# Attention scores and softmax weights turned by VectorE's 32x32 block transposes instead of TensorE's

## The chip, the core and the metric

The kernel runs on one core of one Trainium2 chip. The metric is the device time of one execution in microseconds (us), as the median of several runs. Abbreviations are those of the profile: PE is TensorE (PEld its weight loads), DVE is VectorE, ACT is ScalarE, POOL is GpSimd, SP is SyncE, which issues the DMAs. L12 is line 12 of the kernel.

## The reference

A packed attention is followed by two feed-forward layers. With 8 batches, 8 heads, 576 tokens, 64 features a head and 32 packed queries:

```
sm_attn(qq, kk, vv): s = scale * qq @ kk^T;  s -= max(s);  a = exp(s);  a /= sum(a) + 1e-9;  return a @ vv
p_packed = sm_attn(p, k, v)                      # 32 rows a head
out      = sm_attn(q, p_packed, p_packed)        # 576 rows a head, 32 columns of scores
x = out as (4608 tokens, 512)
x = x / rms(x) * rms_g;  x = (silu(x @ w_gate) * (x @ w_val)) @ w_out     # 512 -> 1536 -> 512
h = x @ w_in;  result = (h * cos(h)) @ w_out2                             # 512 -> 2048 -> 512
```

The second attention has 32 scores for each head and token, and its softmax runs over those 32. The change is about that softmax.

## The kernel before

**Stages.** First come 16 packing units (two a batch, four heads each), which compute `p_packed` from k, v and p, and load and narrow the weights beside it (the L143 to L153 operations on tiles `wy` and `ny`). From its fifth unit on, this stage also carries the second attention of batch 0. Then the first feed-forward layer runs batch by batch, 24 half-blocks a batch: `gv` is gate and value of 128 features for 288 tokens (12 matmuls, three for each product, since each operand is split into a high and a low part), `acc` adds the product with `w_out` (6 matmuls, three half-blocks later). Between the half-blocks of batch b lies the second attention of batch b+1. The last batch has no attention beside it. Then comes the second feed-forward layer (`hp`, `ops`).

**The attention** of a batch is a generator, `attend`, that yields between small steps. For each group g of four heads it turns q on TensorE (`qtp`), multiplies by the packed rows (`sp`, 128 rows of head and packed query x 288 tokens, one tile for even and one for odd tokens), and copies the two tiles out (`sT`, one by ScalarE, one by VectorE). It turns them on TensorE (`stp`, blocks of 96 tokens x 128), takes maxima over 32 scores (`amx`) and subtracts. After both groups `s` holds 96 partitions x 1536; two exponentials, then two rounds of sum, reciprocal and scaling (`sm`) work on halves of 768 columns. Then the weights are turned back by TensorE, four blocks of three transposes (`atp`), each copied by ScalarE into `at`. The steps x (products `xp` and squares for the norm), r, b and p follow.

**What sets the order.** The program is written out by hand in these two stages. In the packing stage each unit takes up to three steps of `attend(0)`, `ATT_U` in all. In the feed-forward layer `att_step` takes steps in proportion: `N_ATT` steps over the 48 half-steps of a batch. After the softmax the order of steps is a string, `ATT_ORD` (`ATT_ORD0` for batch 0), in which `t` turns weights, `x`, `r`, `b`, `p` are as above and `-` is an empty step:

```
ATT_ORD = "t00 t10 - x00 t01 t11 - x10 - - r00 - - b00 b10 p00 p10"
ATT_ORD0 = "t00 t10 x00 x01 t01 t11 x10 x11 - r00 - b00 b10 p00 p10"
```

The matmul outputs of attention, of `gv` and of `unit` (tile `mps`, which makes the folded weights `wmhl` of a batch) share one PSUM pool: `psb[0]`, two buffers in the packing stage and four in the feed-forward layer. ScalarE holds one table of functions at a time: silu and exp need a table load (ACT_TABLE_LOAD) between them.

Of the kernel before, what the change touches and what calls it, by code (L numbers as in the profile page):

```python
# [9 lines left out]
F32 = mybir.dt.float32  # L10
F32R = mybir.dt.float32r
I32 = mybir.dt.int32  # L12
AF = mybir.ActivationFunctionType
# [7 lines left out]
def kernel(  # L21
# [14 lines left out]
    nc = tc.nc  # L36
# [28 lines left out]
    W_FROM, W_TO = 1, 16  # L65
    W_ORD = (0, 1, 2, 3, 16, 4, 5, 6, 17, 7, 8, 18, 9, 10, 11, 19, 12, 13, 14)
    W_KV = 16
    ATT_U, U_ATT = 31, 5
    S_PAD = 11
    U_S = {6: 0, 10: 1, 14: 2}  # L70
    U_AT = {3: (0, 3), 8: (0, 4), 14: (0, 5), 16: (1, 0), 18: (1, 1), 20: (1, 2), 22: (1, 3), 26: (1, 4), 30: (1, 5)}
# [6 lines left out]
    T_END, F3_B, OWN = 2, 3, 16  # L78
    LAG, LAG_B = 3, 4

    ATT_ORD = "t00 t10 - x00 t01 t11 - x10 - - r00 - - b00 b10 p00 p10"
    ATT_ORD0 = "t00 t10 x00 x01 t01 t11 x10 x11 - r00 - b00 b10 p00 p10"
    AL_AT, CL_AT = 16, 21
    ATT_FROM, ATT_TO, ATT_FROM0, ATT_TO0, N_ATT = 0, 48, 10, 45, 37
    BX, BS, BW = 10, 13, 12

    wide = w_gate.dtype != F32
# [128 lines left out]
        nc.sync.dma_start(out=cl, in_=c_dram[b])  # L216

    def attend(b):
        s = a1.tile([CP, NC_, H, NP], F32, tag="s", name="s")
        for g in range(2):  # L220
            qTs = []
            for j in (2 * g, 2 * g + 1):
                qv = qn.pop(4 * b + j)
                qT = a2.tile([128, 2, HALF], F32, tag="qT", name="qT")
                for i in range(2):
                    tp = psb[0].tile([128, HALF], F32, tag="mm", name="qtp")
                    for c in range(CH):
                        nc.tensor.transpose(  # L228
                            tp[:, c * CP:(c + 1) * CP], qv[:, i, 2 * c:2 * c + 2, :].rearrange("p c d -> p (c d)"),
                            ident[:CP, :CP],  # L230
                        )
                    nc.scalar.activation(out=qT[:, i], in_=tp, func=AF.Copy)
                    qTs.append(qT[:, i])
                    if i == 0:
                        yield
                load_q()
                yield
            sp = [psb[0].tile([128, HALF], F32, tag="mm", name="sp") for _ in range(2)]
            for h in range(4):
                for r, rows in enumerate((top, bot)):  # L240
                    nc.tensor.matmul(
                        sp[r][h * NP:(h + 1) * NP], bq[rows, 4 * g + h], qTs[h][rows], start=True, stop=True
                    )
            sT = a1.tile([128, 2, HALF], F32, tag="sT", name="sT")
            nc.scalar.activation(out=sT[:, 0], in_=sp[0], func=AF.Copy)
            nc.vector.tensor_copy(sT[:, 1], sp[1])
            yield
            for r in range(2):
                st_p = psb[0].tile([CP, CH, 4, NP], F32, tag="mm", name="stp")
                for c in range(CH):  # L250
                    nc.tensor.transpose(
                        st_p[:, c].rearrange("p h n -> p (h n)"), sT[:, r, c * CP:(c + 1) * CP], ident
                    )
                mx = a2.tile([CP, CH, 4], F32, tag="amx", name="amx")
                nc.vector.tensor_reduce(out=mx, in_=st_p, op=ALU.max, axis=AX.X)
                nc.vector.tensor_tensor(
                    out=s.rearrange("p (c t) h n -> p c t h n", t=2)[:, :, r, 4 * g:4 * g + 4, :], in0=st_p,
                    in1=mx.unsqueeze(3).to_broadcast([CP, CH, 4, NP]), op=ALU.subtract,
                )
            yield  # L260
        n_s = 8 * CH
        hv = [s[:, hf * CH:(hf + 1) * CH].rearrange("p c h n -> p (c h) n") for hf in range(2)]
        for sf in hv:
            nc.scalar.activation(out=sf, in_=sf, func=AF.Exp, scale=scale)
            yield "e"
        for sf in hv:
            sm = a2.tile([CP, 2, n_s], F32, tag="sm", name="sm")
            nc.vector.tensor_reduce(out=sm[:, 0], in_=sf, op=ALU.add, axis=AX.X)
            nc.vector.tensor_scalar(out=sm[:, 0], in0=sm[:, 0], scalar1=1e-9, scalar2=None, op0=ALU.add)
            nc.vector.reciprocal(out=sm[:, 1], in_=sm[:, 0])  # L270
            yield
            if b:
                yield
            nc.vector.tensor_tensor(
                out=sf, in0=sf, in1=sm[:, 1].unsqueeze(2).to_broadcast([CP, n_s, NP]), op=ALU.mult
            )
            yield

        def transposed(hf, kt):
            tp = psb[0].tile([128, HALF], F32, tag="mm", name="atp")  # L280
            for c in range(CH):
                nc.tensor.transpose(
                    tp[:, c * CP:(c + 1) * CP],
                    s[:, hf * CH + c, 4 * kt:4 * kt + 4, :].rearrange("p h n -> p (h n)"), ident[:CP, :CP],
                )
            return tp

        z = {}

        def a_t(hf, kt):  # L290
            if (hf, kt) == (0, 0):
                z["at"] = a1.tile([128, 2, 2, HALF], F32, tag="at", name="at")
            nc.scalar.activation(out=z["at"][:, kt, hf], in_=transposed(hf, kt), func=AF.Copy)

        def a_x(kt, part):
            at = z["at"]
# [708 lines left out]
    def o_out(n, t):  # L1005
# [8 lines left out]
        while off < 128:  # L1014
            if n < B:
                b, u = n, t * 128 + off
            else:
                b, u = divmod(t * 128 + off, REST)
                u += TOK
            c, pp = divmod(u, CP)  # L1020
            m = min(128 - off, CP - pp)
            dst = out[b * S:(b + 1) * S].rearrange("(p c) d -> c p d", c=NC_)[c, pp:pp + m, :]
            nc.sync.dma_start(out=dst, in_=ob[off:off + m])
# [57 lines left out]
```

## Time and profile before

| | |
|---|---|
| median of 3 runs | 1689.0 us (1687.13 to 1690.26) |
| span of the profiled execution, first to last instruction | 1681.2 us |
| TensorE busy | 1628.8 us, 97% of the span |
| VectorE busy | 1008.5 us, 60% |
| ScalarE busy | 845.2 us, 50% |
| GpSimd busy | 73.9 us, 4% |

The profiled execution has a time of its own only as its span; the runs' times take in what lies around the span. Busy time of matmuls is modelled from starts, as they are pipelined: where the distance between two starts matters, the timeline shows it. A shape such as 96x384 is partitions x elements. "Idle before" is the time the engine stood still just ahead of the instructions of a group, and the arrow names what ended it. The granted clock is TensorE's, as a share of full speed.

### The profile page before, as it was taken

The page shows a single profiled execution, that of the slowest core. Times are in us where ns is not written, and L with a number is a line of the kernel's source. Part 1 is how long each engine was busy: PE and PEld are TensorE (multiplying, and loading weights), DVE is VectorE, ACT ScalarE, POOL GpSimd, SP SyncE. Part 2 cuts the span into 40 slices and gives each one's busy share as a digit, 9 for nine tenths or more (in the row PEclk, how much of TensorE's full clock was granted, in tenths as well). Part 3 has the DMA queues.
Part 4 walks back from the last instruction along what each step waited for, and adds up shares of the span by engine and source line. Part 5 has one row for each costly group of instructions (what it writes and reads, how often), then busy time and mean ns, then how long its engine had stood idle before and what let it go on. Part 6 is the DMA issues. An engine that isn't in the chain of part 4 may idle for free.

```text
span 1681.2 us, 26128 instructions
## 1 busy us (share of the span) xinstructions
PE 1628.8 (97%) x10112; PEld 1325.8 (79%) x10112; DVE 1008.5 (60%) x1890; ACT 845.2 (50%) x1587; POOL 73.9 (4%) x74
## 2 busy tenths in 40 slices
PE   7877999999999999999999999999999999999998
PEld 5545868788888788888888888888888888888887
DVE  3577985566565666665435665656565656565554
ACT  4455555455454545454434554545454545454443
POOL 1001430000000000000110000000000000000000
PEclk9887999999999999999999999999999999999999
DMA  9996744454535454544363020101010101000001
GB/s 253 285 247 173 226 158 153 145 183 139 195 120 179 143 176 144 170 127 131 104 239 106 25 63 1 51 1 51 0 50 1 50 1 41 11 0 26 1 26 25
DMA packets 103580, 177.35 MB, mean 105 GB/s; under 512 B 39456, under 2 KB 55840, under 8 KB 103456
## 3 DMA queue, kind: packets, MB, share of 16 engines
q1 hardware_dynamic: 103456, 175.68, 34.4%
q8 instruction: 80, 1.31, 0.3%
q14 instruction: 44, 0.36, 0.1%
HBM read 134.22 MB, written 41.42 MB: 104 GB/s over the span
## 4 chain that ended last, share of the span: by engine, by line
PE 89%; DMA 5%; DVE 3%; ACT 1%; issue 1%; SPq 1%; POOL 0%; DVEq 0%; POOLq 0%; ACTq 0%
PE hp L160 8%; PE hp L159 8%; PE hp L158 8%; PE ops L160 8%; PE ops L159 8%; PE ops L158 8%; PE gv L158 6%; PE acc L158 6%; PE gv L159 6%; PE gv L160 6%; PE acc L160 6%; PE acc L159 6%; PE mps L580 3%; DMA kn<-in_k_dram 2%; PE qtp L228 1%
## 5 line engine op out<-in xcount | busy, mean ns | idle before, releaser
L158 PE MATMUL gv<-apt,wmhl 128*128 128x288 f32 x768 | 237.8, 310 | 3.0 <-DVE silu L766 2.0
L159 PE MATMUL gv<-apt,wmhl 128*128 128x288 f32 x768 | 228.6, 298 | 0.2 <-DVE apt L107 0.2
L160 PE MATMUL gv<-apt,wmhl 128*128 128x288 f32 x768 | 228.0, 297 | 0.0
L159 PE MATMUL hp<-xhl,wmhl 128*128 128x512 f32 x576 | 224.1, 389 | 0.0
L160 PE MATMUL hp<-xhl,wmhl 128*128 128x512 f32 x576 | 224.1, 389 | 0.0
L158 PE MATMUL ops<-w2hl,ghl 128*128 128x512 f32 x576 | 224.1, 389 | 0.0
L159 PE MATMUL ops<-w2hl,ghl 128*128 128x512 f32 x576 | 224.1, 389 | 0.0
L158 PE MATMUL hp<-xhl,wmhl 128*128 128x512 f32 x576 | 223.9, 389 | 0.0
L160 PE MATMUL ops<-w2hl,ghl 128*128 128x512 f32 x576 | 222.3, 389 | 0.0
L981 ACT ACTIVATE r<-r 128x512 f32<-128x512 f32 x144 | 91.1, 633 | 250.0 <-DVE r L980 250.0
L989 DVE TENSOR_TENSOR r<-r,hp 128x512 f32<-128x512 f32 x144 | 98.9, 687 | 164.8 <-ACT r L982 164.8
L158 PEld LDWEIGHTS gv<-apt,wmhl 128*128 128x128 f32 x768 | 146.0, 190 | 44.3 <-issue 17.6
L158 PE MATMUL acc<-shl,wohl 128*128 128x512 f32 x432 | 176.6, 409 | 0.2 <-DMA shl<-s 0.2
L160 PE MATMUL acc<-shl,wohl 128*128 128x512 f32 x432 | 170.7, 395 | 2.4 <-POOL wohl L546 2.4
L159 PE MATMUL acc<-shl,wohl 128*128 128x512 f32 x432 | 169.6, 393 | 0.0
L773 ACT ACTIVATE shl<-silu 128x288 fp32r<-128x288 f32 x192 | 85.4, 445 | 159.6 <-DVE silu L766 158.4
L766 DVE TENSOR_TENSOR silu<-silu,gv 128x288 f32<-128x288 f32 x192 | 86.5, 451 | 125.5 <-PE gv L160 106.2
L976 ACT ACTIVATE kk<-hp,magic 128x512 f32<-128x512 f32 x144 | 99.1, 688 | 117.3 <-PE hp L160 117.1
L159 PEld LDWEIGHTS gv<-apt,wmhl 128*128 128x128 f32 x768 | 146.2, 190 | 4.4 <-DVE apt L107 0.5
L160 PEld LDWEIGHTS gv<-apt,wmhl 128*128 128x128 f32 x768 | 145.8, 190 | 0.0
L977 DVE TENSOR_SCALAR kk<-kk 128x512 f32<-128x512 f32 x144 | 61.4, 426 | 116.1 <-ACT kk L976 116.0
L158 PEld LDWEIGHTS ops<-w2hl,ghl 128*128 128x128 f32 x576 | 108.2, 188 | 22.6
(127 smaller groups left out, 2708.4 us busy)
## 6 DMA issues: line engine op xcount, KB each, us to landing
wy<-wy SPq DMA_DIRECT2D x96, 512.0 KB, 4.5
kn<-in_k_dram SPq DMA_DIRECT2D x16, 576.0 KB, 7.4
vn<-in_v_dram SPq DMA_DIRECT2D x48, 192.0 KB, 6.5
qnat<-in_q_dram SPq DMA_DIRECT2D x32, 288.0 KB, 4.1
x_dram<-x SPq DMA_DIRECT2D x18, 512.0 KB, 3.0
x1raw<-x_dram SPq DMA_DIRECT2D x18, 512.0 KB, 4.0
raw<-in_moe_w_in_dram SPq DMA_DIRECT2D x16, 512.0 KB, 4.2
raw<-in_moe_w_out_dram SPq DMA_DIRECT2D x16, 512.0 KB, 4.2
```

The source lines that it names most:

```text
L158: nc.tensor.matmul(ps, lhi, rhi, start=first, stop=False)
L159: nc.tensor.matmul(ps, lhi, rlo, start=False, stop=False)
L160: nc.tensor.matmul(ps, llo, rhi, start=False, stop=last)
L228: nc.tensor.transpose(tp[:, c * CP:(c + 1) * CP], qv[:, i, 2 * c:2 * c + 2, :].rearrange("p c d -> p (c d)"), ident[:CP, :CP],)
L580: nc.tensor.matmul(ps[kt][h * NP:(h + 1) * NP], ppT[b // 4][rows, 4 * kt + h, n:n + NP], w_y[2 * u + kt][rows, j], start=True, stop=True,)
L766: nc.vector.tensor_tensor(out=t, in0=t, in1=pss[1], op=ALU.mult)
L773: nc.scalar.activation(out=sh[:, 0, cols], in_=t, func=AF.Copy)
L976: nc.scalar.activation(out=kk, in_=hp, func=AF.Identity, scale=1.0 / TWO_PI, bias=magic[:, 0:1])
L977: nc.vector.tensor_scalar(out=kk, in0=kk, scalar1=-MAGIC, scalar2=None, op0=ALU.add)
L981: nc.scalar.activation(out=r, in_=r, func=AF.Abs)
L989: nc.vector.tensor_tensor(out=r, in0=r, in1=hp, op=ALU.mult)
```

## The change

The score tiles stay with 128 rows. VectorE's transpose works inside blocks of 32 x 32: a tile of 128 rows (4 heads x 32 packed queries) x 288 tokens becomes one whose partition is head and token-within-block and whose columns are block and packed query. So the 32 scores of a head and token stand side by side on one partition, and the softmax runs on 128 partitions x 576 for each group. One exponential covers both groups (128 x 1152). The same transpose turns the weights back into `at`, whose columns then hold the even tokens and then the odd ones; the output's row mapping follows (line with `CH` in `o_out`). TensorE's `stp` and `atp` and the copies `sT` and `at` are gone. The steps of the generator become 28 (batch 0, before its last two) and 32.

```diff
-    ATT_U, U_ATT = 31, 5
+    ATT_U, U_ATT = 28, 5
-    ATT_ORD = "t00 t10 - x00 t01 t11 - x10 - - r00 - - b00 b10 p00 p10"
-    ATT_ORD0 = "t00 t10 x00 x01 t01 t11 x10 x11 - r00 - b00 b10 p00 p10"
+    ATT_ORD = "t00 - x00 t10 - x10 - - r00 - - b00 b10 p00 p10"
+    ATT_ORD0 = "t00 x00 x01 t10 x10 x11 - r00 - b00 b10 p00 p10"
-    ATT_FROM, ATT_TO, ATT_FROM0, ATT_TO0, N_ATT = 0, 48, 10, 45, 37
+    ATT_FROM, ATT_TO, ATT_FROM0, ATT_TO0, N_ATT = 0, 48, 10, 45, 32
...
-        s = a1.tile([CP, NC_, H, NP], F32, tag="s", name="s")
+        NB = HALF // NP
+        s = a1.tile([128, 2, 2, NB, NP], F32, tag="s", name="s")
...
-            sT = a1.tile([128, 2, HALF], F32, tag="sT", name="sT")
-            nc.scalar.activation(out=sT[:, 0], in_=sp[0], func=AF.Copy)
-            nc.vector.tensor_copy(sT[:, 1], sp[1])
+            st = a2.tile([128, 2, NB, NP], F32, tag="st", name="st", bufs=1)
+            for r in range(2):
+                nc.vector.transpose(st[:, r].rearrange("p c n -> p (c n)"), sp[r])
             yield
-            for r in range(2):
-                st_p = psb[0].tile([CP, CH, 4, NP], F32, tag="mm", name="stp")
-                for c in range(CH):
-                    nc.tensor.transpose(
-                        st_p[:, c].rearrange("p h n -> p (h n)"), sT[:, r, c * CP:(c + 1) * CP], ident
-                    )
-                mx = a2.tile([CP, CH, 4], F32, tag="amx", name="amx")
-                nc.vector.tensor_reduce(out=mx, in_=st_p, op=ALU.max, axis=AX.X)
...
+            mx = a2.tile([128, 2 * NB], F32, tag="amx", name="amx")
+            nc.vector.tensor_reduce(out=mx, in_=sv, op=ALU.max, axis=AX.X)
+            nc.vector.tensor_tensor(
+                out=s[:, g].rearrange("p r c n -> p (r c) n"), in0=sv,
+                in1=mx.unsqueeze(2).to_broadcast([128, 2 * NB, NP]), op=ALU.subtract,
+            )
             yield
-        for sf in hv:
-            nc.scalar.activation(out=sf, in_=sf, func=AF.Exp, scale=scale)
-            yield "e"
-        for sf in hv:
-            sm = a2.tile([CP, 2, n_s], F32, tag="sm", name="sm")
+        nc.scalar.activation(out=s, in_=s, func=AF.Exp, scale=scale)
+        yield "e"
+        for g in range(2):
+            sf = s[:, g].rearrange("p r c n -> p (r c) n")
+            sm = a2.tile([128, 2, 2 * NB], F32, tag="sm", name="sm")
...
-            if b:
-                yield
...
-        def a_t(hf, kt):
-            if (hf, kt) == (0, 0):
+        def a_t(kt, _):
+            if kt == 0:
                 z["at"] = a1.tile([128, 2, 2, HALF], F32, tag="at", name="at")
-            nc.scalar.activation(out=z["at"][:, kt, hf], in_=transposed(hf, kt), func=AF.Copy)
+            nc.vector.transpose(
+                z["at"][:, kt].rearrange("p r x -> p (r x)"), s[:, kt].rearrange("p r c n -> p (r c n)")
+            )
...
+            c = 2 * (c % CH) + c // CH
```

How instructions move is shown at three places; a row is one instruction or a run of equal ones, with output, inputs and output shape. First TensorE in the feed-forward layer of batch 1, at the score product of batch 2's first group. Before:

```order
L241 MATMUL sp<-qT,bq 32x288 x8
L158 MATMUL acc<-shl,wohl 128x512
L159 MATMUL acc<-shl,wohl 128x512
L160 MATMUL acc<-shl,wohl 128x512
L158 MATMUL acc<-shl,wohl 128x512
L159 MATMUL acc<-shl,wohl 128x512
L160 MATMUL acc<-shl,wohl 128x512
L251 MATMUL stp<-ident,sT 96x128 x6
L158 MATMUL gv_3366<-apt,wmhl 128x288
```

After:

```order
L158 MATMUL acc<-shl,wohl 128x512
L159 MATMUL acc<-shl,wohl 128x512
L160 MATMUL acc<-shl,wohl 128x512
L158 MATMUL acc<-shl,wohl 128x512
L159 MATMUL acc<-shl,wohl 128x512
L160 MATMUL acc<-shl,wohl 128x512
L242 MATMUL sp<-qT,bq 32x288 x8
L158 MATMUL gv_3270<-apt,wmhl 128x288
```

`stp` is gone, and `sp` has moved from ahead of the `acc` block to behind one. Second ScalarE in the same loop, at the exponential of batch 2. Before, from the first exponential's table load:

```order
L264 ACT_TABLE_LOAD
L264 ACTIVATE s<-s 96x768
L773 ACTIVATE shl<-silu 128x288
L765 ACT_TABLE_LOAD
L765 ACTIVATE silu<-gv_3611 128x288
```

After:

```order
L750 ACTIVATE silu<-gv_3477 128x288
L758 ACTIVATE shl<-silu 128x288
L257 ACT_TABLE_LOAD
L257 ACTIVATE s<-s 128x1152
L750 ACT_TABLE_LOAD
L750 ACTIVATE silu<-gv_3503 128x288
```

Before, such a sequence stands twice in a batch, once for each half; after, it stands once, and the copy `shl` has moved ahead of it. Third the packing stage, TensorE at the last units that carry batch 0's attention (`pp` ends a unit's packing product, `et` and `s` open the next one's). Before:

```order
L282 MATMUL atp<-ident,s 128x96 x3
L460 MATMUL pp<-vn,eT 32x64 x24
L302 MATMUL xp<-at,cl 64x288 x8
L446 MATMUL et<-ident,e 128x128 x6
L423 MATMUL s_1641<-kT,pT 32x288 x8
```

After:

```order
L445 MATMUL pp<-vn,eT 32x64 x24
L287 MATMUL xp<-at,cl 64x288 x4
L431 MATMUL et<-ident,e 128x128 x6
L408 MATMUL s_1503<-kT,pT 32x288 x8
```

and VectorE beside it, after (`cd` reads `pp`, `at` is read by `xp`):

```order
L266 TENSOR_TENSOR s<-s,sm 128x576
L449 TENSOR_SCALAR cd<-pp,mx 128x128
L276 STREAM_TRANSPOSE at<-s 128x576
L297 TENSOR_TENSOR ssq<-ssq,sq 128x288
L143 TENSOR_SCALAR ny<-ny 128x512
```

The turn of the weights has moved from TensorE, a unit step ahead of `xp`, to VectorE, behind `cd` and directly ahead of `xp`.

## Rows read from the trace of the kernel before

**Rows 1.** Busy time by stretch: start:end, length, engines, granted clock, DMA share, GB/s.
```profile
100.00:165.00 65.00, 44.86 (x568) 31.20 (x569) 46.26 (x108) 34.05 (x81) 2.88 (x4) 0.76 0.72 202
165.00:265.00 100.00, 93.65 (x683) 72.85 (x681) 82.21 (x146) 55.12 (x120) 39.22 (x25) 0.98 0.57 178
265.00:805.00 540.00, 540.00 (x3996) 441.59 (x3988) 328.87 (x690) 279.12 (x591) 9.51 (x6) 1.00 0.48 155
```
**Rows 2.** TensorE's groups, 265 to 805 us: busy us, mean ns, idle before.
```profile
L158 PE MATMUL gv<-apt,wmhl 128*128 128x288 f32 x592 | 182.4, 308 | 0.0
...
L282 PE MATMUL atp<-ident,s 96*128 96x96 f32 x72 | 9.9, 245 | 0.0
L251 PE MATMUL stp<-ident,sT 128*96 128x128 f32 x72 | 9.8, 272 | 0.0
```
**Rows 3.** TensorE's timeline from 724 us: start, duration, instruction (L159, L160 left out).
```profile
724.77 0.82 PE L251 MATMUL stp<-ident,sT 128*96 128x128 f32 x6
725.34 0.38 PE L158 MATMUL gv<-apt,wmhl 128*128 128x288 f32 x1
...
727.01 0.39 PE L158 MATMUL acc<-shl,wohl 128*128 128x512 f32 x1
...
728.40 0.29 PE L158 MATMUL gv<-apt,wmhl 128*128 128x288 f32 x1
...
729.99 0.40 PE L158 MATMUL acc<-shl,wohl 128*128 128x512 f32 x1
...
744.45 0.41 PE L282 MATMUL atp<-ident,s 96*128 96x96 f32 x3
744.64 0.38 PE L158 MATMUL gv<-apt,wmhl 128*128 128x288 f32 x1
...
746.32 0.41 PE L282 MATMUL atp<-ident,s 96*128 96x96 f32 x3
```
**Rows 4.** VectorE's groups by shape, whole span.
```profile
L255 DVE TENSOR_REDUCE amx<-stp 96x12 f32<-96x384 f32 x32 | 17.6, 548 | 12.7 <-PE stp L251 12.7
...
L274 DVE TENSOR_TENSOR s<-s,sm 96x768 f32<-96x768 f32 x16 | 15.2, 948 | 0.0
...
L268 DVE TENSOR_REDUCE sm<-s 96x24 f32<-96x768 f32 x16 | 15.1, 941 | 0.0
...
L334 DVE TENSOR_TENSOR at<-at,rb 128x576 f32<-128x576 f32 x16 | 11.7, 749 | 0.0
...
L246 DVE COPY sT<-sp 128x288 f32<-128x288 f32 x16 | 7.2, 451 | 1.0 <-PE sp L241 1.0
...
L270 DVE RECIPROCAL sm<-sm 96x24 f32<-96x24 f32 x16 | 4.8, 299 | 0.6
...
L269 DVE TENSOR_SCALAR sm<-sm 96x24 f32<-96x24 f32 x16 | 3.1, 193 | 0.5
```
**Rows 5.** ScalarE's groups by shape, 265 to 805 us.
```profile
L264 ACT ACT_TABLE_LOAD x12 | 15.4, 1283 | 0.2
...
L264 ACT ACTIVATE s<-s 96x768 f32<-96x768 f32 x12 | 10.2, 848 | 0.1
L293 ACT ACTIVATE at<-atp 128x288 f32<-128x288 f32 x24 | 9.8, 410 | 5.2 <-PE atp L282 5.1
```
**Rows 6.** Timeline from 197 us, ScalarE's silu and TensorE's waits (in brackets).
```profile
197.01 0.41 ACT L765 ACTIVATE silu<-gv 128x288 f32<-128x288 f32 x1 [1.32 <-PE gv L160]
...
203.14 0.41 ACT L765 ACTIVATE silu<-gv 128x288 f32<-128x288 f32 x1
...
209.31 0.44 PE L282 MATMUL atp<-ident,s 96*128 96x96 f32 x3 [1.32 <-ACT silu L765]
...
212.80 0.61 PE L158 MATMUL gv<-apt,wmhl 128*128 128x288 f32 x1 [2.03 <-DVE silu L766]
```
**Rows 7.** Waits, 100 to 168 us: who for whom, us in total, times, longest.
```profile
PE xp L302 <- ACT at L293: 3.5, 2, 2.0
PE mps L580 <- ACT sq L311: 3.5, 1, 3.5
```

More of the change, by code (lines that the diff above doesn't have):

```diff
@@ L243, in attend @@
                     )
-            sT = a1.tile([128, 2, HALF], F32, tag="sT", name="sT")
-            nc.scalar.activation(out=sT[:, 0], in_=sp[0], func=AF.Copy)
-            nc.vector.tensor_copy(sT[:, 1], sp[1])
+            st = a2.tile([128, 2, NB, NP], F32, tag="st", name="st", bufs=1)
+            for r in range(2):
+                nc.vector.transpose(st[:, r].rearrange("p c n -> p (c n)"), sp[r])
             yield
-            for r in range(2):
-                st_p = psb[0].tile([CP, CH, 4, NP], F32, tag="mm", name="stp")
-                for c in range(CH):
-                    nc.tensor.transpose(
-                        st_p[:, c].rearrange("p h n -> p (h n)"), sT[:, r, c * CP:(c + 1) * CP], ident
-                    )
-                mx = a2.tile([CP, CH, 4], F32, tag="amx", name="amx")
-                nc.vector.tensor_reduce(out=mx, in_=st_p, op=ALU.max, axis=AX.X)
[L256 to L259, printed above, removed]
-            yield
-        n_s = 8 * CH
-        hv = [s[:, hf * CH:(hf + 1) * CH].rearrange("p c h n -> p (c h) n") for hf in range(2)]
-        for sf in hv:
-            nc.scalar.activation(out=sf, in_=sf, func=AF.Exp, scale=scale)
-            yield "e"
-        for sf in hv:
-            sm = a2.tile([CP, 2, n_s], F32, tag="sm", name="sm")
+            sv = st.rearrange("p r c n -> p (r c) n")
+            mx = a2.tile([128, 2 * NB], F32, tag="amx", name="amx")
[4 more added lines that the diff above has]
+            )
+            yield
+        nc.scalar.activation(out=s, in_=s, func=AF.Exp, scale=scale)
[3 more added lines that the diff above has]
+            sm = a2.tile([128, 2, 2 * NB], F32, tag="sm", name="sm")
             nc.vector.tensor_reduce(out=sm[:, 0], in_=sf, op=ALU.add, axis=AX.X)
@@ L271, in attend @@
             yield
-            if b:
-                yield
             nc.vector.tensor_tensor(
-                out=sf, in0=sf, in1=sm[:, 1].unsqueeze(2).to_broadcast([CP, n_s, NP]), op=ALU.mult
+                out=sf, in0=sf, in1=sm[:, 1].unsqueeze(2).to_broadcast([128, 2 * NB, NP]), op=ALU.mult
             )
             yield
[L279 to L286, printed above, removed]
         z = {}
-        def a_t(hf, kt):
-            if (hf, kt) == (0, 0):
+        def a_t(kt, _):
+            if kt == 0:
                 z["at"] = a1.tile([128, 2, 2, HALF], F32, tag="at", name="at")
-            nc.scalar.activation(out=z["at"][:, kt, hf], in_=transposed(hf, kt), func=AF.Copy)
+            nc.vector.transpose(
+                z["at"][:, kt].rearrange("p r x -> p (r x)"), s[:, kt].rearrange("p r c n -> p (r c n)")
+            )
         def a_x(kt, part):
```

## The prediction

> **What bounds the kernel now.** I read the table of stretches first, since a share over the whole span mixes stages [rows 1]. It shows three regimes ahead of the second feed-forward layer. From 100 to 165 us (end of the packing units, in which batch 0's attention runs) no engine is full: TensorE 44.9 of 65 us, VectorE 46.3, granted clock 0.76. From 165 to 265 us (feed-forward layer of batch 0, with batch 1's attention in between) VectorE is busy 82.2 of 100 us and TensorE 93.7. From 265 to 805 us (batches 2 to 7's attention) TensorE is busy 540.0 of 540 us at a granted clock of 1.00, VectorE 328.9 and ScalarE 279.1.
>
> A busy TensorE is modelled, so the second view is the groups of that stretch with their idle time: the feed-forward matmuls and both transposes that go waited 0.0 us [rows 2]. The third is the timeline, which gives starts. A block of 12 gv matmuls straight after acc takes 728.40 to 729.99, 1.59 us, or 0.13 us each; the starts follow at one distance, without a gap [rows 3].
>
> The Trainium skill (Perfetto Trace Analysis, section Identifying the Most-Contended Engine) speaks against reading this as a bound: busy time of matmuls is no good measure of headroom, because they are pipelined. That rule is weighed by the starts in rows 3, which show back-to-back work; if it nevertheless meant slack here, the sum below would be zero, which is the second rival.
>
> **TensorE's part, step by step.** Two groups go: in each batch 12 score transposes (stp, two blocks of 6) and 12 weight transposes (atp, four blocks of 3); the counts of 72 over six batches in [rows 2] agree. Their durations, 272 and 245 ns, are latencies; what they hold of a full engine is the distance of starts [rows 3]:
> - stp: 724.77 to 725.34 is 0.57 us for six. The gv block behind it takes 725.34 to 727.01, 1.67 us against 1.59: coming back to the feed-forward matmuls costs 0.08 us more. Together 0.65 us.
> - atp: 744.45 to 744.64 is 0.19 us for three, and the gv block behind takes 744.64 to 746.32, 1.68 us: 0.09 more. Together 0.28 us.
>
> A batch thus gives back 2 x 0.65 + 4 x 0.28 = 2.42 us. Six batches lie where TensorE is the bound: 6 x 2.42 = 14.5 us. The q transposes, score products, xp and rb stay in number; in the order some move to the other side of an acc block, which I cost at nothing: as many returns to the feed-forward matmuls remain.
>
> By the Trainium skill (TensorE: Matmul & The Clock Gate, Part 4: PE-mode transpose) a transpose costs about 275 ns in a kernel's context, most of it memory latency. The latency agrees with the 272 ns of rows 2, but charged per instruction it would make 24 x 0.275 = 6.6 us a batch, an estimate from that page; the starts in rows 3 decide for 2.42.
>
> **VectorE's part.** From [rows 4], per batch: out go two score copies (2 x 0.45), four maxima (4 x 0.55), four subtractions (about as long, 4 x 0.55), two sums (2 x 0.94), two scalings (2 x 0.95), together 9.1 us. In come operations on 128 partitions x 576 instead of 96 x 768 or 96 x 384: two maxima, subtractions, sums and scalings, eight at the 0.75 us of the 128x576 row, 6.0 us. Unknown are the transposes: four of 128x288 from PSUM and two of 128x576. No row has one. Low end: what an operation on 24 elements takes, 0.19 us each, 1.2 us in all. High end: the slowest rate per element in the trace, RECIPROCAL against TENSOR_SCALAR on the same 24 elements, (299 - 193)/24 = 4.4 ns above a base of 0.19, giving 0.19 + 288 x 0.0044 = 1.5 us and 2.7 us, so 4 x 1.5 + 2 x 2.7 = 11.4 us. I take the copy of the same shape from PSUM, 0.45, and the 128x576 row, 0.75: 3.3 us, since a transpose without arithmetic streams its columns as a copy does. VectorE ends at 9.3 us a batch, 0.2 more than now; at the high end 8.3 more. In 265 to 805 us that is 6 x 8.3 = 50 us on top of 329 of 540: still not the bound, so there the cover is VectorE's free 39%.
>
> **ScalarE's part.** It loses two score copies and four weight copies (0.41 each, [rows 5]), and two exponentials of 0.85 become one of 128x1152, about 0.85 x 1152/768 = 1.27 us. An exponential between silu's forces two table loads of 1.28 us [rows 5]; in batches 2 to 7 the two exponentials stand on either side of a silu, so four loads become two. All this is hidden now (TensorE waits for nothing in that stretch), so I cost it at nothing there. Against it: the loads and the exponential stand in one piece, 1.28 + 1.27 + 1.28 = 3.8 us against 3.4, and silu behind them frees the PSUM buffers of gv. Counted from the end of a gv block: silu, VectorE's product and the copy take about 0.41 + 0.45 + 0.41 = 1.3 us, the piece lasts until 5.1, the next silu and product until 6.0. That next gv block ended at 1.39 + 1.59 = 2.98, and its buffers are wanted two blocks on, at 2 x 2.98 + 1.39 = 7.35 us. That leaves 1.3 us; today's shorter piece causes no wait.
>
> **Batch 1 (165 to 265 us).** TensorE gives back the same 2.42 us. Here VectorE binds for a while: TensorE waits 1.32 us at 209.31 and 2.03 us at 212.80, the second for VectorE's silu product; on ScalarE no silu ran from 197.4 to 203.1, while both exponentials and their table loads did [rows 6]. In the new order one exponential follows a silu directly and the copy and reload come behind it: between two silu's 1.28 + 1.27 + 0.41 + 1.28 = 4.2 us, against those 5.7. I take 1.4 us of the difference off the 3.35 us wait. The softmax pieces on VectorE are also 0.2 us shorter each, while the two at transposes come later, where it has room; I count neither. Together 3.8 us. At the high end of the transposes four slow ones fall into the full stretch, 4 x 1.05 = 4.2 us later.
>
> **Stage to 165 us (batch 0).** No engine is full behind 100 us, so chains decide [rows 1]. New: the at transposes stand on VectorE behind cd, which needs pp of the same unit, and TensorE's xp stands right behind pp; it waits for cd and the transpose, at least 0.75 us, in two units. Queued behind xp are the et transposes and the packing scores; their maximum comes on VectorE only after four or more narrowing operations on 128x512, each longer than the 0.45 us of a 128x288 copy, so over 1.8 us, which cover the wait. Without that cover it costs 1.5 us, and 3 with as much again for cd and what queues ahead. Gone: xp's waits for the ScalarE copies, 3.5 us, and mps's wait behind the squares, 3.5 us [rows 7], as mps no longer stands right behind four xp. If a good half of these 7 was on the chain, 4 us go. I take the middle, about 0, between -4 and +3; at the high end of the transposes 2 x 1.95 = 3.9 more.
>
> **The sum.** -14.5 - 3.8 + 0 = -18.3 us. The profiled execution spans 1681.2 us, so 1662.9; the median of the runs is 1689.0, 7.8 above that span, for what lies around it and for differences between executions; I carry that over: 1670.7 us.
>
> **Rivals.**
> 1. The transposes are slow. For: no row shows one. Against: VectorE has room from 265 us on. Time at the high end: -18.3 + 4.2 + 3.9 = -10.2, 1678.8 us; with stage one at its own worst 1682.
> 2. TensorE is not what holds the end: other waits fill the freed time and it goes the same, 1689 us. For: the 3.35 us wait of batch 1. Against: 0.0 idle over 540 us [rows 2]. The Trainium skill's rule on busy time, above, points to this case.
> 3. Slower: the combined exponential holds ScalarE so long, and the VectorE sums queued right behind it wait so long, that the gv buffers come free late in every batch. For: it already happens once, at 3.35 us, in batch 1, where VectorE is full. Price if each of seven batches pays that: 7 x 3.35 = 23.5 us, of which 3.35 are paid now and 1.4 of them counted as gained; -18.3 + 1.4 + 20.1 = +3.2, 1692 us. It decides from 18.3/7 = 2.6 us a batch. Against: batches 2 to 7 have VectorE 61% busy, and 1.3 us in hand.
> 4. Faster still: the waits of batch 1 vanish (2 us more) and stage one gives its 4 us: 1664.7 us.
>
> **Numbers.** Forecast 0.66 (own range 1667 to 1676), slow transposes 0.12, no change 0.06, slower 0.07, faster still 0.09. A difference under 0.2%, 3.4 us, can't be told from none here. So faster by more than 0.2%: 0.66 + 0.12 + 0.09 = 0.87; within 0.06; slower 0.07. The range that leaves a fifth out: 1665 to 1682 us.
>
> **What would show it.** Between 265 us and the end of attention TensorE still has 0.0 us idle, the stretch from the second batch to the seventh is 14 to 15 us shorter, no gv row waits for silu. STREAM_TRANSPOSE takes near 0.45 and 0.75 us. ACT_TABLE_LOAD falls from 13 to 7 for exp. The TensorE waits around batch 1's softmax fall from 3.35 to about 2 us. Wrong would be: transposes beyond 1.5 us, gv waiting 2.6 us or more in each batch, or xp waiting so long in the first stage that batch 0 starts its feed-forward over 3 us later than now.

## The result, and the profile after

| | before | after |
|---|---|---|
| median of the runs of this comparison | 1688.07 us (1686.39 to 1690.26, 4 runs) | 1665.72 us (1664.33 to 1667.76, 4 runs) |
| ratio | | 0.9868 [0.9854, 0.9882] |
| span of the profiled execution | 1681.2 us | 1662.8 us |

The forecast was 1670.7 us, range 1665 to 1682: faster, as forecast, by 22 us rather than 18. The median lies 0.7 us inside that range and 1.3 us below the forecast's own range, 1667 to 1676. The profiled spans differ by 18.4 us, the predicted 18.3; that agreement is partly luck, since the profiled execution of before had a short packing stage, as the first experiment shows.

To see where the time went I cut each trace at the first `gv` matmul of each batch. The table gives the distances between these starts, in us: the packing stage, then the feed-forward loops, each with the attention of the next batch in it. The last loop has none, and the second feed-forward layer, behind it, is 788.2 us in every trace.

| | packing | loop with attention of batch 1 | of batches 2 to 7 | sum of these six | last loop |
|---|---|---|---|---|---|
| before | 154.7 | 99.1 | 88.2, then 87.95 five times | 528.0 | 111.2 |
| after | 155.6 | 94.8 | 85.7, then 85.4 five times | 512.6 | 111.5 |
| difference | +0.9 | -4.3 | -2.55 each | -15.4 | +0.3 |
| predicted | 0 | -3.8 | -2.42 each | -14.5 | 0 |

The same stretches in the changed kernel's trace (columns as in [rows 1], the second and third ends shifted with the work):

```profile
100.00:165.00 65.00, 43.71 (x559) 30.75 (x560) 45.78 (x109) 33.44 (x78) 2.25 (x5) 0.74 0.83 225
165.00:261.00 96.00, 90.65 (x654) 69.76 (x660) 83.56 (x147) 52.07 (x113) 40.42 (x25) 1.00 0.59 188
261.00:786.00 525.00, 525.00 (x3860) 429.59 (x3860) 327.45 (x690) 248.46 (x538) 10.54 (x6) 1.00 0.49 159
```

TensorE still fills the third stretch, 525.0 of 525 us. ScalarE is down from 52% to 47% of it; VectorE is at 62% against 61%. The TensorE groups of that stretch have no `stp` and no `atp` any more, and none of those left waits:

```profile
L158 PE MATMUL gv<-apt,wmhl 128*128 128x288 f32 x592 | 179.8, 304 | 0.0
...
L287 PE MATMUL xp<-at,cl 32*64 32x288 f32 x192 | 8.9, 426 | 0.0
```

VectorE's groups over the whole span, the two transposes first (columns as in [rows 4]):

```profile
L247 DVE STREAM_TRANSPOSE st<-sp 128x288 f32<-128x288 f32 x32 | 13.6, 461 | 7.0 <-PE sp L242 7.0
L276 DVE STREAM_TRANSPOSE at<-s 128x576 f32<-128x576 f32 x16 | 12.3, 769 | 0.0
L251 DVE TENSOR_REDUCE amx<-st 128x18 f32<-128x576 f32 x16 | 12.0, 747 | 0.2
```

The transposes take 461 and 769 ns, where 0.45 and 0.75 us were taken from rows of the same shape; the softmax operations take 0.75 us as assumed. ScalarE:

```profile
L257 ACT ACTIVATE s<-s 128x1152 f32<-128x1152 f32 x8 | 9.3, 1167 | 1.9 <-DVE s L252 1.9
L257 ACT ACT_TABLE_LOAD x7 | 9.0, 1283 | 0.1
```

One exponential is 1.17 us (estimate 1.27), and the table loads for exp fall from 13 to 7.

### The profile page after: what moved, and what is told of

Same layout as the page of the kernel before. It is cut to its first block, busy times and chain, and to the rows that moved or that the text cites. A ratio compares the mean times of both kernels' runs of the same rounds, so it can differ in the third digit from the quotient of the medians.

```text
span 1662.8 us, 25654 instructions
## 1 busy us (share of the span) xinstructions
PE 1607.7 (97%) x9920; PEld 1308.2 (79%) x9920; DVE 1006.9 (61%) x1890; ACT 809.6 (49%) x1519; POOL 74.9 (5%) x74
## 4 chain that ended last, share of the span: by engine, by line
PE 89%; DVE 4%; DMA 3%; ACT 1%; issue 1%; POOL 0%; SPq 0%; DVEq 0%; ACTq 0%; POOLq 0%
PE hp L159 8%; PE hp L160 8%; PE hp L158 8%; PE ops L160 8%; PE ops L159 8%; PE ops L158 8%; PE gv L158 6%; PE acc L158 6%; PE gv L159 6%; PE acc L160 6%; PE gv L160 6%; PE acc L159 6%; PE mps L565 3%; DMA c<-cd 2%; PE qtp L229 1%
## 5 line engine op out<-in xcount | busy, mean ns | idle before, releaser
L159 PE MATMUL gv<-apt,wmhl 128*128 128x288 f32 x768 | 227.8, 297 | 0.4 <-DVE apt L107 0.4
L160 PE MATMUL gv<-apt,wmhl 128*128 128x288 f32 x768 | 226.8, 295 | 0.0
L159 PE MATMUL hp<-xhl,wmhl 128*128 128x512 f32 x576 | 224.1, 389 | 0.0
L160 PE MATMUL hp<-xhl,wmhl 128*128 128x512 f32 x576 | 224.1, 389 | 0.0
L159 PE MATMUL ops<-w2hl,ghl 128*128 128x512 f32 x576 | 224.1, 389 | 0.0
L160 PE MATMUL ops<-w2hl,ghl 128*128 128x512 f32 x576 | 222.3, 389 | 0.0
L758 ACT ACTIVATE shl<-silu 128x288 fp32r<-128x288 f32 x192 | 85.4, 445 | 201.6 <-DVE silu L751 201.6
L160 PE MATMUL acc<-shl,wohl 128*128 128x512 f32 x432 | 170.4, 394 | 2.8 <-POOL wohl L531 2.8
L159 PE MATMUL acc<-shl,wohl 128*128 128x512 f32 x432 | 169.6, 393 | 0.0
L961 ACT ACTIVATE kk<-hp,magic 128x512 f32<-128x512 f32 x144 | 99.1, 688 | 117.4 <-PE hp L160 117.2
L159 PEld LDWEIGHTS gv<-apt,wmhl 128*128 128x128 f32 x768 | 145.0, 189 | 5.9 <-DVE apt L107 0.6
L160 PEld LDWEIGHTS gv<-apt,wmhl 128*128 128x128 f32 x768 | 144.9, 189 | 0.0
L159 PEld LDWEIGHTS ops<-w2hl,ghl 128*128 128x128 f32 x576 | 108.2, 188 | 22.6
```

What stands on the lines that cost most here:

```text
L159: nc.tensor.matmul(ps, lhi, rlo, start=False, stop=False)
L160: nc.tensor.matmul(ps, llo, rhi, start=False, stop=last)
L758: nc.scalar.activation(out=sh[:, 0, cols], in_=t, func=AF.Copy)
L961: nc.scalar.activation(out=kk, in_=hp, func=AF.Identity, scale=1.0 / TWO_PI, bias=magic[:, 0:1])
```

## The experiments

### Before again: what lies around the span

The kernel before, unchanged, timed in more rounds.

> The kernel before once more, to read its span beside its time in several executions. Of the change the medians show 22.3 us, the two profiled spans 18.4. Theory A (the profiled execution of before was a short one): the runs of before have spans of about 1684 to 1688 us, some 2 us under their times as in the kernel after, and vary by 2 to 4 us in the packing stage, while first gv to end varies by under 1 us. Theory B (before has 6 us more around its span): spans stay near 1681 with times near 1688.

Measured: 1686.27 us (1682.69 to 1689.41, 10 runs), ratio 0.9998 [0.9988, 1.0008]. In every run the time is 2.1 to 2.2 us above that run's span; the changed kernel's nine runs are 1.8 above theirs. The 7.8 us that I carried over as one amount were therefore some 2 us around the span, a profiled execution that happened to be short, and three runs that were somewhat long (1689.0 us, against medians of 1686.3 to 1688.1 in the later series). The second trace shows where the difference lies: 157.6 us of packing instead of 154.7, and every later loop within 0.2 us of the first trace. If that rest is constant (1526.5 and 1526.6 us in the two traces), the packing stage of each run is its span less 1526.6: over the 41 runs of the kernel before whose spans the experiments give, 153.9 to 162.8 us, median 158.1. The same for the changed kernel, with 1507.0: nine runs, 150.4 to 159.0, median 155.8. So its profiled packing of 155.6 is an ordinary one, that of before a short one, and the change takes 2 to 3 us from this stage. That the rest is constant is an assumption; one trace below, of the kernel with both shifts, departs from it by 2.6 us.

### The TensorE transposes put back, unread

In batches 1 to 7 the 24 transposes of a batch run again on TensorE, into PSUM tiles that nothing reads; all else is the changed kernel.

```diff
             sv = ...
+            for r in range(2 if b else 0):
+                st_p = psb[0].tile([CP, CH, 128], F32, tag="mm", name="stp")
+                for c in range(CH):
+                    nc.tensor.transpose(st_p[:, c], st[:, r]...[:, c * CP:(c + 1) * CP], ident)
...
         def a_t(kt, _):
+            for hf in range(2 if b else 0):
+                at_p = psb[0].tile([128, HALF], F32, tag="mm", name="atp")
+                for c in range(CH):
+                    nc.tensor.transpose(at_p[:, c * CP:(c + 1) * CP], s[:CP, kt]...[:, c * 128:(c + 1) * 128], ident[:CP, :CP])
```

> The changed kernel, with TensorE transposes put back beside VectorE's in batches 1 to 7: 6 of 128x96 behind each group's score transpose and 6 of 96x128 behind each weight transpose, into PSUM tiles that nobody reads. Theory A (the gain of the full stretch is TensorE's start distances and returns): a batch costs 2 x (0.57 + 0.08) + 2 x (0.39 + 0.09) = 2.26 us, about 14 us from 261 us on and 16 us in all. Theory B (the gain came from ScalarE and VectorE having less to do): under 4 us.

Measured: 1680.11 us (1677.64 to 1681.11, 4 runs), ratio to before 0.9962 [0.9947, 0.9977], 14.4 us above the changed kernel. The six loops sum to 527.5 us, 2.5 more each: nearly all of what the change gave there. TensorE's groups between 266 and 794 us of this run:

```profile
L253 PE MATMUL stp<-ident,st 128*96 128x128 f32 x72 | 9.8, 272 | 0.0
L288 PE MATMUL atp<-ident,s 96*128 96x96 f32 x72 | 8.2, 248 | 0.1
```

Their modelled busy time, 18.0 us, is more than the 14.9 us that they cost, which the distances of starts gave (14.5). The Trainium skill (TensorE: Matmul & The Clock Gate, Part 4: PE-mode transpose) gives about 275 ns for a transpose (128x128 bf16) in one kernel's context; the durations of these fp32 transposes are near it (272 and 248 ns), but as the cost in a full engine it would be 24 x 0.275 = 6.6 us a batch, an estimate from that page, and the run shows 2.5. The loop with batch 1 is only 1.2 us longer, half of the 2.42 us that the prediction took for this loop as well: most of its 4.3 us gain is not the start distances of these transposes.

### Every VectorE transpose three times

```diff
-                nc.vector.transpose(st[:, r]..., sp[r])
+                for _ in range(3):
+                    nc.vector.transpose(st[:, r]..., sp[r])
...
+            for _ in range(3):
                 nc.vector.transpose(z["at"][:, kt]..., s[:, kt]...)
```

This adds 8 x 0.46 + 4 x 0.77 = 6.8 us of VectorE work to each batch, and asks whether VectorE's free share covers it.

> The changed kernel with each of VectorE's block transposes issued three times: per batch 4 x 2 x 0.46 + 2 x 2 x 0.77 = 6.8 us more of VectorE, near the high end of the prediction. Theory A (VectorE has room from batch 2 on and binds only ahead of that): 0 us from 261 us on, 3 to 8 us in the packing stage and batch 1. Theory B (VectorE is near its bound everywhere): up to 6 x 6.8 = 41 us more.

Measured: 1697.9 us (1695.77 to 1699.38, 4 runs), ratio to before 1.0069 [1.0054, 1.0084]: slower than before. Against the changed kernel the packing stage is some 6 us longer (161.4 us in the median of the runs against 155.8), batch 1's loop 6.7, and each of the six loops 3.5 (533.9 in sum). Its stretch and its TensorE waits between 270 and 790 us (engine, line, what was waited for: us in total, times, longest):

```profile
265.00:795.00 530.00, 517.27 (x3745) 417.50 (x3745) 360.06 (x750) 241.12 (x527) 11.82 (x7) 1.00 0.48 155
```

```profile
PE xp L289 <- DVE at L278: 5.7, 5, 1.3
PE gv L158 <- DVE silu L753: 3.2, 6, 0.7
PE xp L289 <- DVE silu L753: 2.3, 6, 0.6
```

VectorE is busy 360 of 530 us, 68%, and yet half of what it got in addition shows in the time. The prediction's cover, "VectorE's free 39%", does not exist as such.

### Only the weight transposes three times

As above, in `a_t` alone and in batches 1 to 7 (`range(3 if b else 1)`): 3.1 us of VectorE work a batch.

> The changed kernel with only the weight transposes (128x576) issued three times, in batches 1 to 7: 3.1 us more of VectorE a batch. With all transposes tripled the batches cost 3.4 us more each, mostly as xp waiting for VectorE. Theory A (xp is near enough to the transpose that VectorE's delay shows): 1 to 2 us a batch. Theory B (the score transposes hold PSUM and so gv): under 0.3 us a batch.

Measured, one run: 1676.18 us; the six loops sum to 521.3, 1.4 us more each, and the loop with batch 1 takes 97.0 us against 94.8. One place of it in the timeline (start, duration, engine, line, operation, idle time before it and what ended it):

```profile
303.10 2.39 DVE L277 STREAM_TRANSPOSE at<-s 128x576 f32<-128x576 f32 x3
...
304.04 0.41 ACT L751 ACTIVATE silu<-gv 128x288 f32<-128x288 f32 x1 [0.38 <-PE gv L160]
...
305.64 0.71 PE L288 MATMUL xp<-at,cl 32*64 32x288 f32 x6 [0.20 <-DVE at L277]
...
306.35 0.45 DVE L752 TENSOR_TENSOR silu<-silu,gv 128x288 f32<-128x288 f32 x1
...
306.85 0.72 PE L288 MATMUL xp<-at,cl 32*64 32x288 f32 x10 [0.51 <-DVE silu L752]
```

The transposes end at 305.49, and `xp` waits 0.20 us for them. It waits 0.51 more in its middle: its four outputs come from the pool whose buffers `gv` uses, and one of these is free only after VectorE's silu product at 306.35, ready since silu ended at 304.45 but queued behind the transposes and two further operations. The cover is the time until the next reader and the next buffer to be freed: a single transpose would have ended at 303.87, 1.57 us before `xp` was due at 305.44. The mean share says nothing of it.

### The same with the reader a step later

The order string moves each `xp` one step away from its transposes, by a `-` taken from further on.

```diff
-    ATT_ORD = "t00 - x00 t10 - x10 - - r00 - - b00 b10 p00 p10"
+    ATT_ORD = "t00 - - x00 t10 - - x10 - r00 - b00 b10 p00 p10"
```

> As the kernel with tripled weight transposes, with one more empty step between each turn and its xp in batches 2 to 7 (t00 - - x00 t10 - - x10 - r00 - b00 b10; as many steps as before), which puts another half-block between them. With tripled transposes a batch took 86.8 us against 85.4, and its xp blocks 1.14 us in the median against 0.67. Theory A (the cover is the distance between the transpose and the matmuls that read it or need a buffer freed behind it): xp blocks are back at 0.67 us and a batch at 85.4 to 85.7 us, though VectorE works as much. Theory B (VectorE's total work costs): a batch stays near 86.8.

Measured, one run: 1670.29 us. The six loops sum to 513.7, 0.17 more each than in the changed kernel, with the same tripled transposes. Its stretch:

```profile
265.00:795.00 530.00, 530.00 (x3884) 433.19 (x3883) 348.82 (x719) 249.85 (x542) 9.08 (x6) 1.00 0.49 158
```

TensorE is full again, and VectorE is busier than in the run before it (348.8 against 344.5 us of 530): in these loops distance to the reader decides. The order string holds for batch 1 too, and there the step does not help: its loop takes 98.4 us, against 97.0 with the tripled transposes alone and 94.8 in the changed kernel. VectorE is nearly full there (34.1 of 35 us from 180 to 215 us in the changed kernel), and in both tripled runs TensorE's granted clock is at 0.50 for some 3.4 us of that loop, which the next section takes up.

### Two exponentials, as before

```diff
-        nc.scalar.activation(out=s, in_=s, func=AF.Exp, scale=scale)
-        yield "e"
+        for g in range(2):
+            nc.scalar.activation(out=s[:, g], in_=s[:, g], func=AF.Exp, scale=scale)
+            yield "e"
```

with a step more in `ATT_U` (29) and `N_ATT` (33).

> The changed kernel with two exponentials a batch again, one for each group, a step apart. Theory A (merging them matters only where VectorE is full): 0 us in batches 2 to 7 although six pairs of table loads come back (15 us of ScalarE), and 0 to 2 us in batch 1. Theory B (the merged exponential is a large part of the gain): 5 us or more slower.

Measured: 1662.03 us (1660.19 to 1663.1, 4 runs), ratio 0.9856 [0.9841, 0.987]. The table loads are back, and in the six loops (513.4 in sum) they cost 0.1 us each:

```profile
L258 ACT ACT_TABLE_LOAD x14 | 18.0, 1283 | 0.2
L258 ACT ACTIVATE s<-s 128x576 f32<-128x576 f32 x16 | 11.0, 687 | 0.2
```

Batch 1's loop is 2.0 us longer (96.9 us). It goes with a lower clock: TensorE starts the seventeenth half-block of this loop 0.3 us earlier than in the changed kernel and the eighteenth 2.05 us later, and in between its granted clock is 0.50, the lower of its two levels (1.2 GHz). These are the stretch of this run and the one at the same distance from the loop's start in the changed kernel (columns as in [rows 1]):

```profile
209.90:213.30 3.40, 3.40 (x15) 3.26 (x14) 2.69 (x6) 1.15 (x3) 1.81 (x1) 0.50 0.52 210
```

```profile
215.40:218.80 3.40, 3.40 (x21) 2.90 (x20) 2.71 (x6) 2.10 (x6) 1.24 (x1) 1.00 0.34 135
```

Whether the second exponential brought the lower clock about is not shown. Nevertheless the time is not longer than the changed kernel's: the packing stage is 150.1 us in its trace and 150.3 in the median of its runs. The edit does two things there: it splits batch 0's exponential, and it puts in a further step, which moves the weight transposes and `xp` to other places of the units. That led to the next three.

### Weight transposes and xp of batch 0 at other steps

```diff
-    ATT_U, U_ATT = 28, 5
-    ATT_ORD0 = "t00 x00 x01 t10 x10 x11 - r00 - b00 b10 p00 p10"
# xp a step behind its transposes:
+    ATT_U, U_ATT = 30, 5
+    ATT_ORD0 = "t00 - x00 x01 t10 - x10 x11 - r00 - b00 b10 p00 p10"
# all a step later:
+    ATT_U, U_ATT = 29, 5
+    ATT_ORD0 = "- t00 x00 x01 t10 x10 x11 - r00 - b00 b10 p00 p10"
# both:
+    ATT_U, U_ATT = 31, 5
+    ATT_ORD0 = "- t00 - x00 x01 t10 - x10 x11 - r00 - b00 b10 p00 p10"
```

xp a step behind:

> The changed kernel with an empty step between the turn of the weights and xp in the packing stage (steps t00 - x00 x01 t10 - x10 x11). In the changed kernel's profile TensorE waited 7.7 us there for VectorE's transposes, 5.1 in one piece. Theory A (that wait is on the chain): it goes, and the packing stage is 2 to 5 us shorter. Theory B (VectorE's narrowing operations cover it, as predicted): the wait goes and the time stays within 1 us. From the first gv on nothing changes.

All a step later:

> The changed kernel with its one exponential, and one empty step ahead of the turn of the weights in the packing stage, which puts t00 and x00 where the kernel with two exponentials has them. That kernel's packing stage was 5.5 us shorter, its batch 1 2.1 us longer. Theory A (the shifted steps, not the second exponential, shortened the packing stage): packing near 150 to 152 us and batch 1 as in the changed kernel, 94.8 us, so about 4 to 6 us faster than it. Theory B (two shorter exponentials help there, or the first loads happened to land early): no more than 1 us.

Both:

> The changed kernel with both shifts of the packing stage at once: an empty step ahead of the turn and one behind each turn (- t00 - x00 x01 t10 - x10 x11 - r00 - b00 b10). One shift alone gave 1660.2 and 1659.3 us against 1664.0 of the changed kernel. Theory A (each takes away the same wait for the transpose): 1658 to 1661 us, no more than one alone. Theory B (they add): 1655 us or less.

The changed kernel once more, beside these:

> The changed kernel once more, on the same chip as the others, for its packing stage in another execution: 154 to 158 us if that stage varies as before's does, and a ratio to before of 0.986 to 0.988.

| | median us | ratio to before | packing, median of the runs |
|---|---|---|---|
| changed kernel again | 1663.96 (1659.16 to 1667.16, 5 runs) | 0.986 [0.9839, 0.988] | 155.4 |
| xp a step behind | 1660.19 (1658.52 to 1670.48, 6 runs) | 0.9852 [0.9826, 0.9878] | 151.3 |
| all a step later | 1659.3 (1657.66 to 1662.86, 4 runs) | 0.9837 [0.9816, 0.9857] | 150.6 |
| both | 1662.12 (1658.67 to 1665.78, 4 runs) | 0.9857 [0.9828, 0.9885] | 151.1 |

(Packing is again each run's span less the rest of its own trace.) What the shifts by one step take away is this, TensorE's longest waits from 85 to 165 us in the changed kernel:

```profile
PE xp L287 <- DVE at L276: 7.7, 2, 5.1
PE et L431 <- ACT e L420: 3.7, 2, 2.8
PE rp L303 <- DVE ssq L297: 2.5, 1, 2.5
```

and with xp a step behind its transposes:

```profile
PE et L431 <- ACT e L420: 5.0, 2, 4.1
PE rp L303 <- DVE wmhl L107: 3.1, 1, 3.1
PE xp L287 <- ACT sq L296: 3.0, 1, 3.0
```

The wait for `at` is gone, and the others have grown somewhat. With both shifts 3.0 us of it are left. By the medians of the runs the shifts take 4 to 5 us from the packing stage, but a single trace does not show it: the changed kernel once more had a longer wait for `at` and yet a packing stage of only 150.6 us (154 to 158 were expected).

```profile
PE xp L287 <- DVE at L276: 9.0, 2, 6.4
```

What differs between the two traces of the changed kernel lies ahead of this wait: at the first `xp` they are 5.0 us apart (112.70 and 107.67 us), at the first `gv` 5.1. So the kernels are compared better from a fixed point of the stage. From the tenth of its sixteen `tp` matmuls (at 105.09 us in the changed kernel) to the first `gv` it is 51.7 us in both traces of before; 50.0 to 51.4 in the five traces whose packing stage is the changed kernel's (that kernel twice, the one with transposes put back, and the two with tripled weight transposes); and 47.8 to 48.6 in the four with a shift, the two exponentials among them. On average the shifts give 2.5 us there, a third of the 7.7 us of waits, and both together (48.4) no more than one. Since a later step with one exponential does as much as the kernel with two (48.1 and 47.8), the step shortened the stage there, not the second exponential. The rest of the 4 to 5 us lies ahead of that point and is not explained.

Both together is also slower than its packing tells, by another cause. Its loop with batch 1 holds the same instructions in the same order on TensorE, VectorE, ScalarE and GpSimd as the changed kernel's and takes 97.4 us instead of 94.8, and in it TensorE's granted clock is at the lower level for 6.8 us:

```profile
205.40:212.20 6.80, 6.43 (x33) 4.84 (x34) 4.78 (x9) 2.86 (x7) 2.22 (x2) 0.50 0.47 188
```

From the fifth half-block up to that stretch the `gv` starts of the two loops agree within 0.05 us. So the median of this kernel lies above the 1658 to 1661 us expected, and the reason need not be its packing. The intervals of the ratios overlap, and the run-to-run spread of the packing stage is as large as the gain. The fastest kernel here by its median, with all a step later, is 1.6% under the kernel before.

## Why the prediction was right, and where it was not

**TensorE's part was right.** 2.42 us a batch from distances of starts and returns, 2.55 measured, and 2.5 come back when the transposes do. The second rival (nothing changes, since a busy TensorE need not be full) fell with it. The Trainium skill (Perfetto Trace Analysis, section Identifying the Most-Contended Engine) says that the busy share of matmuls is no good measure of how close TensorE is to its limit; here the idle time of 0.0 and the even starts of [rows 2, 3] had shown that no time was free.

**Durations were right.** 461 and 769 ns against 0.45 and 0.75 us taken by shape.

**Batch 1: the number was right, its parts were not.** 4.3 us against 3.8. TensorE's waits from 165 to 262 us in the changed kernel:

```profile
PE acc L160 <- POOL wohl L531: 2.8, 5, 0.6
PE acc L158 <- ACT wohl L528: 0.9, 1, 0.9
...
PE gv L158 <- DVE silu L751: 0.8, 1, 0.8
```

Of the 3.35 us in [rows 6] 0.8 are left, not 2. But the wait for ScalarE's `wohl` (0.9 us) is new, and that for GpSimd's has grown by 0.4, so that from the fifth half-block of the loop on (up to there the two kernels run level) TensorE's waits fall from 5.7 to 4.5 us in all. ScalarE's rows there:

```profile
199.67 0.41 ACT L750 ACTIVATE silu<-gv 128x288 f32<-128x288 f32 x1 [0.46 <-PE gv L160]
200.10 1.28 ACT L257 ACT_TABLE_LOAD   x1
201.39 1.17 ACT L257 ACTIVATE s<-s 128x1152 f32<-128x1152 f32 x1
202.87 0.45 ACT L758 ACTIVATE shl<-silu 128x288 fp32r<-128x288 f32 x1 [0.31 <-DVE silu L751]
203.33 1.28 ACT L750 ACT_TABLE_LOAD   x1
204.62 0.41 ACT L750 ACTIVATE silu<-gv 128x288 f32<-128x288 f32 x1
```

From the end of one silu to the start of the next are 4.5 us, against 5.7 before and 4.2 worked out. The working took the 5.7 us for the exponentials, their loads and the copy; these lines of the kernel before stood in them too, and in the changed kernel the same two operations on weights stand ahead of the silu:

```profile
200.64 0.62 ACT L543 ACTIVATE wohl<-ny 128x512 fp32r<-128x512 f32 x1
201.16 0.66 ACT L133 ACTIVATE ny<-wo 128x512 f32<-128x512 f32 x1
```

They are 1.2 us, as much as the stretch became shorter; whether that or VectorE's queue shortened the wait no run tells apart. A third part was not in the working at all. From the end of the 2.03 us wait of [rows 6] on, TensorE's granted clock is at the lower level in the kernel before, and so it is in its second trace:

```profile
212.55:215.96 3.41, 3.16 (x13) 3.14 (x14) 2.98 (x5) 2.54 (x6) 0.86 (x1) 0.50 0.52 135
```

There the block of twelve `gv` matmuls takes 3.05 us, 212.80 to 215.85, instead of 1.6, with starts 0.24 us apart instead of 0.13: about 1.4 us. Four of the five traces with the changed kernel's loop have no such stretch behind the first half-blocks; the fifth, the one with both shifts, pays 2.6 us for its own. So the gain here holds fewer waits (1.2 us), a clock that did not fall (about 1.4), and the transposes, of whose 2.42 us only 1.2 came back when they were put back; that the sum met 3.8 is partly luck. The third rival (the merged exponential holds up `gv` in every batch) did not come: `gv` waits 0.0 us in the six loops.

**The high end of the transposes: the step that failed.** The working put 8.3 us more of VectorE work a batch under "VectorE's free 39%" and so gave slow transposes 1678.8 us, still faster than before. Tripling them (6.8 us a batch) gave 1697.9, slower than before. The forecast held because the transposes are as fast as assumed; the first rival stood on the wrong side. What hides VectorE work in the six full loops is the stretch until its reader and until the next buffer that its queue must free.

**Packing stage: the place was right, the wait was not.** The wait for `at` was seen as at least 0.75 us twice, and the working held that the narrowing operations on VectorE "cover the wait". The trace of the changed kernel, at the first of the two:

```profile
107.51 0.69 DVE L149 SCALAR_TENSOR_TENSOR wy<-wo,wy 128x512 int32<-128x512 int32 x1
108.24 0.69 DVE L153 SCALAR_TENSOR_TENSOR wy<-wo,wy 128x512 int32<-128x512 int32 x1
108.85 0.69 DVE L531 TENSOR_TENSOR wohl<-ny,wohl 128x512 fp32r<-128x512 f32 x1
...
110.95 0.75 DVE L266 TENSOR_TENSOR s<-s,sm 128x576 f32<-128x576 f32 x1
111.61 0.34 DVE L449 TENSOR_SCALAR cd<-pp,mx 128x128 f32<-128x128 f32 x1
...
111.88 0.77 DVE L276 STREAM_TRANSPOSE at<-s 128x576 f32<-128x576 f32 x1
...
112.70 1.23 PE L287 MATMUL xp<-at,cl 32*64 32x288 f32 x8 [5.05 <-DVE at L276]
...
114.72 0.46 DVE L297 TENSOR_TENSOR ssq<-ssq,sq 128x288 f32<-128x288 f32 x1 [2.08 <-ACT sq L296]
```

Some narrowing operations are part of this wait: they stand ahead of the transpose in VectorE's queue and fill its first 1.9 us, to 109.54. Then come the packing's own maximum, the scaling of the softmax, `cd` and the transpose. Those that were to cover it, behind `xp`, begin only at 115.10: in VectorE's queue they stand behind `ssq`, which needs the squares of what `xp` makes, and VectorE stood idle 2.08 us for it. So they start later with `xp` instead of hiding its wait. (The four take 2.2 us, and two of them 0.42 and 0.43, not over 0.45 as the working had it.) The second wait, 2.61 us, has no narrowing operation in it; there VectorE itself waited for ScalarE's squares:

```profile
121.29 1.02 DVE L297 TENSOR_TENSOR ssq<-ssq,sq 128x288 f32<-128x288 f32 x2 [2.35 <-ACT sq L296]
122.23 0.34 DVE L449 TENSOR_SCALAR cd<-pp,mx 128x128 f32<-128x128 f32 x1
122.49 0.77 DVE L276 STREAM_TRANSPOSE at<-s 128x576 f32<-128x576 f32 x1
...
123.40 1.24 PE L287 MATMUL xp<-at,cl 32*64 32x288 f32 x8 [2.61 <-DVE at L276]
```

The working priced the two waits at 1.5 to 3 us without cover; they measured 7.7, and the shifted orders got 2.5 of them back behind the fixed point. The stage came out 2 to 3 us shorter all the same, within the -4 to +3 given; which of the waits that went accounts for it no run tells apart.

**From the span to the median, and the term that was mis-sized.** The 7.8 us were carried over from one execution, but since the span and the 7.8 us add up to the median of before, the forecast is that median less 18.3 us, and the step moved nothing. What the one execution hid is the packing stage (154.7 us against a median of 158.1): it was put at 0 in the sum and gave 2 to 3 us by the medians. With 19.3 us from the first `gv` on and 0.3 around the span that is some 22 us, as between the measured medians. The fourth rival (the waits of batch 1 vanish and the packing stage gives 4 us, 1664.7) comes nearest to the measured 1665.7: a good half of both came.

## What to carry to other kernels

Price a matmul that goes by the distance of starts and the return to the work behind it, in a stretch where TensorE's groups wait 0.0. Price work added to another engine by what its queue must still do before the next reader, and before the next buffer comes free: an engine with a third of its time free can cost half of all that is added, and one step of distance to the reader can make it free where its queue is not full. Read the granted clock of a stretch before naming the cause of its length. Take the step from span to median from the spans of several runs, and ask which stage varies.

## What was not expected of the hardware

- One exponential instead of two saves 14 table loads of 1283 ns (two in each of seven loops), and that was worth 0.1 us in each of the six loops that TensorE fills. The 2.0 us in the loop with batch 1 go with a stretch of 3.4 us at the lower granted clock.
- The same instructions in the same order took 94.8 us in four traces and 97.4 us in a fifth, which has 6.8 us at a granted clock of 0.50 in that loop. What made it fall there is not shown: from the loop's fifth half-block up to there TensorE's `gv` starts agree within 0.05 us with the changed kernel's.
- The rest of the run-to-run spread sat, as far as the traces tell, in the packing stage, which varies by 9 us over 41 runs of one kernel, and there ahead of 105 us. In that part the DMA share is about 1, and of two traces of a kernel the one with the shorter stage moved more in the same time, though no run shows that this is the cause: 272 and 263 GB/s from 0 to 105 us before (packing 154.7 and 157.6 us), and the changed kernel's two, the second execution (150.6 us) first and then the first (155.6 us), these:

```profile
0.00:105.00 105.00, 81.75 (x1014) 56.43 (x1014) 57.99 (x145) 49.93 (x119) 6.47 (x29) 0.90 1.03 269
0.00:105.00 105.00, 79.36 (x962) 55.43 (x963) 52.96 (x134) 49.41 (x117) 6.26 (x28) 0.89 1.02 252
```

- VectorE's block transpose of fp32 runs at the pace of a copy of its shape: 461 ns for 288 columns from PSUM (a copy took 451, [rows 4]) and 769 for 576 from SBUF. That is 1.07 ns for each further column, if the two sources cost the same, against 0.83 for ScalarE's exponential (687 ns at 576 columns, 1167 at 1152).
